# When the weight conversions stand among the attention tiles: a table of 24 steps redrawn

## The chip, the cores and the metric

The kernel runs on one core of one Trainium2 chip. The metric is the device time of one execution in microseconds (us). The core has five engines that run side by side and wait for one another by semaphores: TensorE (PE in the profile; PEld is its weight load), VectorE (DVE), ScalarE (ACT), GpSimd (POOL) and SyncE (SP), which here issues nearly every DMA.

## What is computed

Three layers follow one another, for B = 4 batches of S = 448 tokens with E = 768 channels (12 heads of 64). q, k, v are float32; all weights are float64 in memory.

```python
attn = softmax(causal(q @ k.T / 8)) @ v          # 4 x 12 heads, 448 x 448 scores
x = attn.reshape(B, S, E)
h = relu(x.T @ w_tok1) @ w_tok2                  # token mixing
u = x + h.T
x = u + relu(u @ w_ch1) @ w_ch2                  # channel mixing, 768 -> 1536 -> 768
theta = x @ w_theta                              # third layer
y = w_tok_r @ (x * cos(theta)) + w_tok_i @ (x * sin(theta))
u = x + y
out = u + relu(u @ w_ch)
```

## The kernel before

**Steps.** The attention is cut into 168 steps: 24 pairs of heads (6 to a batch) by 7 tiles of query rows. One pass of the loop over `steps` writes the scores of step n (`scores`, matmuls in L353, and L355 from step 84), the mask and row maximum on DVE (L360), the exponential on ACT (L362), and four steps later (`LAG`) the product with v (`late_step`, L401 or L412). Up to step 55 the probabilities are turned on PE (L369); from step 56 by a DMA transpose from `ph` to `pt` in SP's queue (L385). After every second pair the token mixing runs (L436 to L455).

**Units.** The channel mixing is cut into 96 units of 18 matmuls (L231 to L233): 24 for a batch, of which 0 to 5 and 12 to 17 belong to `w_ch1`, the others to `w_ch2`. Unit 0 starts at step `FIRST_UNIT` = 53; there is a unit about every 2.5 steps up to step 88 and then one about every 1.45 steps, so that unit 23 is due at step 102. A unit's weights are a tile of 384 KB in HBM (`wd`, w_c in the profile), loaded by `load_unit` (L226) up to three units ahead.

**Conversions.** Those 24 tiles must first be made out of the float64 weights, once, in the order of the first 24 units. This is the list `ROUNDINGS`: pairs (step, n), where n < 0 are the four tiles of the token mixing at steps 3, 4, 8, 9, and n = 0 to 23 are the tiles of the channel mixing. A conversion that stands at step s does this:

- step s: `round_first`: the high words are copied on ACT (L177) and their sign is cut out on POOL (L130, `raw`)
- step s + 1: `round_bits`: two bit operations on DVE (L185, L186), and the squares of the rows on ACT (L124)
- step s + 2: the `fetch` of the conversion three places later in the list (L173, 768 KB, 3 `raw` buffers)
- step s + 3: `round_split`: a power of two from the squares (`power`: two matmuls of one column, two DVE operations of one column, L140 and L127, two small POOL operations), then the high part on POOL (L163, `ws`) and the low part on DVE (L197, `ws`)
- step s + 5: `round_store`: the tile goes to HBM (L569, 384 KB). Only then may `load_unit` fetch it for its unit.

**Order.** The order on each engine is fixed when the program is built: a scheduler goes by the order of the code, by priorities (the attention is placed 500 instructions ahead by `AHEAD`, conversions and units are not) and by its own estimate of times. On the chip each engine then takes its instructions strictly in that order, and SP its DMAs too. Six late conversions for `w_ch` (`convert_late`) and the third layer come after step 94 in the code and are not touched.

Of the kernel before, what the change touches and what calls it, by code (L numbers as in the profile page):

```python
# [35 lines left out]
FIRST_UNIT, DENSE, RATE = 53, 88, (42, 29)  # L36
UNIT_STEPS = [FIRST_UNIT + n * (DENSE - FIRST_UNIT) // 14 if n < 14 else
              DENSE + -(-(n - 14) * RATE[0] // RATE[1]) for n in range(72)]
ROUNDINGS = [(at_step, n - 4) for n, at_step in enumerate((3, 4, 8, 9))] + [(14 + n * 78 // 23, n) for n in range(24)]
ENGINES = {  # L40
    0: dict(qhi="A", qlo="D", khi="A", klo="D", v="D", phi="A", xhi="A", xlo="D", uhi="A", ulo="D"),
}
# [12 lines left out]
def fused(ctx, tc, q, k, v, w_tok1, w_tok2, w_ch1, w_ch2, w_theta, w_tok, w_ch, out):  # L55
# [124 lines left out]
    def round64(f, raw):  # L180


        low, sign = raw[:, :f.shape[-1], 0], raw[:, :f.shape[-1], 1]
        u = f.bitcast(U32)
        nc.vector.scalar_tensor_tensor(out=u, in0=u, scalar=3, in1=sign, op0=ALU.logical_shift_left, op1=ALU.bitwise_or)  # L185
        nc.vector.scalar_tensor_tensor(out=u, in0=low, scalar=29, in1=u, op0=ALU.logical_shift_right, op1=ALU.bitwise_or)  # L186
# [74 lines left out]
    def tok_weights(n):  # L261
        if n < 2:
            cols = slice(n * 512, (n + 1) * 512)
            return w_tok1[:, cols], wt1[:, :, cols]
        return w_tok2[:, (n - 2) * S:(n - 1) * S], wt2[:, n - 2]
# [273 lines left out]
    def fetch(j):  # L539
        if j < len(ROUNDINGS):  # L540
            n = ROUNDINGS[j][1]
            src = tok_weights(n + 4)[0] if n < 0 else jobs[n][0]
            fetched[j] = src, raw_tile()
            fetch64(*fetched[j])
# [6 lines left out]
    def round_bits(j):  # L551
        n, f = ROUNDINGS[j][1], rounding[j]
        round64(f, fetched.pop(j)[1])
        if n < 0:
            split_w(tok_weights(n + 4)[1], rounding.pop(j))
        else:
            rounding[j] = f, row_squares(f)

    def round_split(j):
        n = ROUNDINGS[j][1]  # L560
        if n >= 0:
            f, sq = rounding.pop(j)
            rounding[j] = ws_tile()
            split_scaled("P", rounding[j], f, jobs[n][2], sq)

    def round_store(j):
        n = ROUNDINGS[j][1]
        if n >= 0:
            nc.sync.dma_start(out=jobs[n][1], in_=rounding.pop(j))  # L569
            stored.add(n)  # L570
# [65 lines left out]
    for n, (b, pr, t) in enumerate(steps):  # L636
# [6 lines left out]
        if n == 0:  # L643
            for j in range(BUFS["raw"]):
                fetch(j)
        for j, (at_step, _) in enumerate(ROUNDINGS):
            if at_step == n - ROUND_BITS:
# [350 lines left out]
```

## Time and profile before

| | us |
|---|---|
| median of 3 runs (876.57 to 880.31) | 880.0 |
| the profiled execution | 880.48 |
| its span, first to last instruction | 878.7 |

The profiled execution is 0.48 us over the median of the runs; 1.8 us of it lie around the span. The rows below all come from that one execution. In a row of windows, "busy" is the time in which an engine had an instruction running, in us of the window, with the number of instructions behind it; PEclk is the granted clock of TensorE as a share of full speed (1.00 is 2.4 GHz, a half is 1.2 GHz); DMA share is the mean busy share of the 16 DMA engines.

### The profile page before, as it was taken

The numbers are of one execution on the slowest core, as the hardware profiler recorded it, in microseconds if no ns is written. First come the engines' busy times: TensorE is split into PE (matmuls) and PEld (weight loads), VectorE is DVE, ScalarE is ACT, GpSimd is POOL, SyncE is SP. The second block draws the span as 40 slices with busy tenths as digits, with TensorE's granted clock in tenths as the row PEclk, the third lists the DMA queues.
The fourth block names the chain that finished last, engine by engine and source line by source line (L and its number), as shares of the span: only waits on it lengthen the run. The fifth ranks groups of instructions, "written<-read, shape, count | busy, mean of one in ns | idle before, by whom it ended". The sixth has DMA issues, their size and how long they took to land.

```text
span 878.7 us, 16252 instructions
## 1 busy us (share of the span) xinstructions
PE 844.2 (96%) x5603; PEld 532.3 (61%) x5603; DVE 611.8 (70%) x1438; ACT 540.1 (61%) x1271; POOL 255.3 (29%) x445
## 2 busy tenths in 40 slices
PE   7999988998989999999999999999999999999997
PEld 6888865566547566665656555555545555555554
DVE  6788797989997666767785358669737448567441
ACT  6797786676856665567755266547636448456441
POOL 4466564447561201222312035341101001101000
PEclk9999999999999999999999999999999999999999
DMA  7856869899699996765574888612612132131011
GB/s 223 259 194 204 265 164 301 232 337 260 160 323 301 287 212 168 199 174 124 160 210 101 251 278 282 219 36 70 198 39 88 48 100 80 56 117 58 19 50 74
DMA packets 122563, 152.01 MB, mean 173 GB/s; under 512 B 78384, under 2 KB 89584, under 8 KB 122480
## 3 DMA queue, kind: packets, MB, share of 16 engines
q1 hardware_dynamic: 121936, 149.95, 58.8%
q0 software_dynamic: 384, 0.79, 0.4%
q8 instruction: 44, 0.72, 0.4%
q14 instruction: 39, 0.32, 0.1%
q10 hardware_dynamic: 160, 0.23, 0.1%
HBM read 110.56 MB, written 22.81 MB: 152 GB/s over the span
## 4 chain that ended last, share of the span: by engine, by line
PE 70%; DMA 12%; DVE 6%; ACT 5%; issue 3%; POOL 2%; SPq 1%; DVEq 0%; ACTq 0%; POOLq 0%
PE ps_mm L231 16%; PE ps_mm L232 16%; PE ps_mm L233 16%; DMA pt<-ph 8%; PE ps_sc L353 4%; PE ps_sc L231 3%; PE ps_sc L232 3%; PE ps_sc L233 3%; DMA ws<-w_c 2%; PE ps_pv L401 2%; ACT junk L124 2%; PE ps_pv L412 2%; DVE ph L382 1%; PE ps_mm L785 1%; PE ps_mm L369 1%
## 5 line engine op out<-in xcount | busy, mean ns | idle before, releaser
L231 PE MATMUL ps_mm<-h,ws 128*128 128x448 f16 x432 | 153.2, 356 | 3.3 <-POOL h L163 1.7
L232 PE MATMUL ps_mm<-h,ws 128*128 128x448 f16 x432 | 153.3, 356 | 1.1 <-DVE g L127 1.0
L233 PE MATMUL ps_mm<-h,ws 128*128 128x448 f16 x432 | 152.8, 355 | 0.0
L233 PEld LDWEIGHTS <-ws 128*128 128x128 f16 x720 | 70.6, 98 | 66.7 <-issue 6.7
L231 PEld LDWEIGHTS <-ws 128*128 128x128 f16 x720 | 70.7, 98 | 65.4 <-issue 3.8
L232 PEld LDWEIGHTS <-ws 128*128 128x128 f16 x720 | 70.7, 98 | 61.9 <-issue 5.4
L362 ACT ACTIVATE sb<-sb,mx 128x320 f32<-128x320 f32 (+3 forms) x168 | 89.3, 533 | 28.0 <-DVE mx L360 27.3
L232 PE MATMUL ps_mm<-ut,ws 128*128 128x448 f16 x288 | 101.5, 353 | 2.4 <-DVE ut L197 2.4
L231 PE MATMUL ps_mm<-ut,ws 128*128 128x448 f16 x288 | 101.2, 353 | 1.5 <-DMA rawt<-x2d 1.3
L233 PE MATMUL ps_mm<-ut,ws 128*128 128x448 f16 x288 | 101.6, 353 | 0.0
L382 DVE SCALAR_TENSOR_TENSOR ph<-sb,ph 128x64 f16<-128x64 f32 (+3 forms) x208 | 64.5, 353 | 32.1 <-ACT ph L160 31.7
L360 DVE CUSTOM_DVE_ANT_0 sb<-ps_sc,mask 128x320 f32<-128x320 f32 (+3 forms) x168 | 74.5, 454 | 14.8 <-PE ps_mm L369 11.4
L160 ACT ACTIVATE ph<-sb 128x192 f16<-128x192 f32 (+3 forms) x112 | 48.4, 442 | 56.3 <-DMA pt<-ph 55.8
L124 ACT ACTIVATE junk<-acc 128x448 bf16<-128x448 f32 x72 | 41.1, 571 | 65.5 <-DVE acc L890 42.7
L353 PE MATMUL ps_sc<-k_pad,q_raw 128*128 128x192 f32 (+3 forms) x168 | 58.8, 451 | 6.0 <-DMA k_pad<-in_k_dram 4.6
L765 POOL TENSOR_SCALAR tmp<-tmp 128x384 f32<-128x384 f32 x28 | 15.5, 555 | 147.4 <-ACT tmp L764 144.3
L163 POOL TENSOR_SCALAR h<-t 128x448 f16<-128x448 f32 x48 | 33.4, 697 | 79.4 <-ACT t L485 78.8
L487 DVE TENSOR_TENSOR h<-t,h 128x448 f16<-128x448 f32 x48 | 32.1, 672 | 23.8 <-POOL h L163 23.7
L231 PE MATMUL ps_sc<-th,ut 128*128 128x384 f16 x144 | 46.9, 326 | 0.0
L233 PE MATMUL ps_sc<-th,ut 128*128 128x384 f16 x144 | 46.8, 326 | 0.0
L232 PE MATMUL ps_sc<-th,ut 128*128 128x384 f16 x144 | 46.6, 326 | 0.0
L130 POOL TENSOR_SCALAR raw<-raw 128x768 f32<-128x768 f32 (+2 forms) x34 | 34.2, 1006 | 40.1 <-ACT wf L177 36.1
(215 smaller groups left out, 2093.8 us busy)
## 6 DMA issues: line engine op xcount, KB each, us to landing
ws<-w_c SPq DMA_DIRECT2D x120, 384.0 KB, 4.5
raw<-in_w_ch_dram SPq DMA_DIRECT2D x30, 768.0 KB, 6.0
w_c<-ws SPq DMA_DIRECT2D x30, 384.0 KB, 3.9
v_raw<-in_v_dram SPq DMA_DIRECT2D x24, 288.0 KB, 3.8
q_raw<-in_q_dram SPq DMA_DIRECT2D x12, 448.0 KB, 4.4
k_raw<-in_k_dram SPq DMA_DIRECT2D x12, 448.0 KB, 5.0
x2d<-acc SPq DMA_DIRECT2D x24, 224.0 KB, 3.6
acc<-x2d SPq DMA_DIRECT2D x24, 224.0 KB, 2.8
```

The source lines that it names most:

```text
L124: nc.scalar.activation(j[:, 0:src.shape[-1]], src, AF.Square, accum_out=dst)
L130: nc.gpsimd.tensor_scalar(out=dst, in0=a, scalar1=b, scalar2=c, op0=ALU.mult, op1=ALU.mult)
L160: nc.scalar.activation(dst, src, AF.Copy, scale=scale)
L163: e.tensor_scalar(out=dst, in0=src, scalar1=scale, scalar2=0.0, op0=ALU.mult, op1=ALU.add)
L231: nc.tensor.matmul(ps, lhsT=ka(a[:, 0]), rhs=kb(b[:, 0]), start=first, stop=False)
L232: nc.tensor.matmul(ps, lhsT=ka(a[:, 0]), rhs=kb(b[:, 1]), start=False, stop=False)
L233: return nc.tensor.matmul(ps, lhsT=ka(a[:, 1]), rhs=kb(b[:, 0]), start=False, stop=last)
L353: nc.tensor.matmul(ps[:, 0:n], lhsT=lhs, rhs=cut(pp.kh), start=True, stop=pp.kl is None)
L360: pp.first = nc.vector.tensor_tensor_reduce(out=dst, in0=src, in1=msk, op0=ALU.add, op1=ALU.min, scale=-0.125, scalar=3.0e38, accum_out=pp ...
L362: pp.last = nc.scalar.activation(sb[:, 0:kk], sb[:, 0:kk], AF.Exp, bias=pp.mx[:, j:j + 1], scale=-1.0, accum_out=pp.sm[:, 2 + j:3 + j])
L382: nc.vector.scalar_tensor_tensor(out=dst, in0=sb[:, c0:c1], scalar=PSC, in1=hi[:, c0:c1], op0=ALU.mult, op1=ALU.subtract)
L487: gates[0] = nc.vector.tensor_tensor(out=t[:, 1], in0=f, in1=t[:, 0], op=ALU.subtract)
```

## The change

The list of steps for n = 0 to 23 is another one; nothing else is touched. Before, the 24 conversions stand at 14, 17, 20, 24, 27, 30, 34, 37, 41, 44, 47, 51, 54, 58, 61, 64, 68, 71, 75, 78, 81, 85, 88, 92. Now they stand at 12, 14, 17, 19, 22, 24, 27, 29, 32, 34, 37, 39, 42 and then at 44, 49, 54, 59, 64, 69, 74, 79, 84, 89, 94.

```diff
-ROUNDINGS = [(at_step, n - 4) for n, at_step in enumerate((3, 4, 8, 9))] + [(14 + n * 78 // 23, n) for n in range(24)]
+ROUNDINGS = [(at_step, n - 4) for n, at_step in enumerate((3, 4, 8, 9))] + [(12 + n * 5 // 2 if n < 13 else 44 + (n - 13) * 5, n) for n in range(24)]
```

The first place is DVE around step 35, from the end of one pair of heads (L418) to the score tile of step 36 (L360, 128x192). Names: `wf` is the tile under conversion, `ws` its finished form, `h` belongs to the token mixing. Before:

```order
L418 RECIPROCAL sm<-sm 128x7
L185 SCALAR_TENSOR_TENSOR wf<-wf,raw 128x768
L440 SCALAR_TENSOR_TENSOR h_913<-ps_mm,h_913 128x256
L186 SCALAR_TENSOR_TENSOR wf<-raw,wf 128x768
L197 SCALAR_TENSOR_TENSOR ws<-wf,s,ws 128x768
L440 SCALAR_TENSOR_TENSOR h_913<-ps_mm,h_913 128x256
L360 ISA sb_186,mx<-ps_sc,mask 128x192
```

Now, from after the same reciprocal on:

```order
L197 SCALAR_TENSOR_TENSOR ws<-wf,s,ws 128x768
L440 SCALAR_TENSOR_TENSOR h_962<-ps_mm,h_962 128x256
L197 SCALAR_TENSOR_TENSOR ws<-wf,s,ws 128x768
L440 SCALAR_TENSOR_TENSOR h_962<-ps_mm,h_962 128x256
L185 SCALAR_TENSOR_TENSOR wf<-wf,raw 128x768
L186 SCALAR_TENSOR_TENSOR wf<-raw,wf 128x768
L185 SCALAR_TENSOR_TENSOR wf<-wf,raw 128x768
L455 TENSOR_TENSOR acc<-ps_mm,acc 128x448 x2
L140 TENSOR_SCALAR g<-ps_mm 128x1
L186 SCALAR_TENSOR_TENSOR wf<-raw,wf 128x768
L360 ISA sb_186,mx<-ps_sc,mask 128x192
```

Three operations of a conversion stood ahead of that score tile; now there are six, and the two additions of the token mixing (L455) stand ahead of it as well.

The second place is SP's queue at the last conversion, n = 23, whose tile is `w_c2_1_5`. Before, the transposes are those of steps 101 to 104:

```order
L385 DMA_TRANSPOSE pt_3699<-ph_3695 128x5x128
L508 DMA x2d0_1_70<-acc_596 128x448
L569 DMA w_c2_1_5_116<-ws_3457 128x1536
L508 DMA x2d0_2_71<-acc_949 128x448
L508 DMA x2d0_3_72<-acc_966 128x448
L173 DMA raw_6615<-in_w_ch_dram 128x1536
L385 DMA_TRANSPOSE pt_3724<-ph_3720 128x5x128
L385 DMA_TRANSPOSE pt_3843<-ph_3839 128x7x128
L385 DMA_TRANSPOSE pt_3887<-ph_3883 128x7x128
L226 DMA ws_3554<-w_c2_1_5_116 128x1536
```

Now, they are those of steps 104 to 107:

```order
L385 DMA_TRANSPOSE pt_3887<-ph_3883 128x7x128
L508 DMA x2d0_2_71<-acc_998 128x448
L508 DMA x2d0_3_72<-acc_1015 128x448
L385 DMA_TRANSPOSE pt_3943<-ph_3940 128x2x128
L385 DMA_TRANSPOSE pt_3975<-ph_3971 128x3x128
L569 DMA w_c2_1_5_116<-ws_3516 128x1536
L385 DMA_TRANSPOSE pt_4020<-ph_4016 128x3x128
L226 DMA ws_3631<-w_c2_1_5_116 128x1536
```

The store of the last tile stood ahead of step 102's transpose and its load behind step 104's; now the store stands behind step 106's and the load behind step 107's. On PE unit 23 itself stands behind the scores of step 111 before and behind those of step 112 now. Between the scores of step 107 and unit 23, PE has 10 matmuls of unit 22 before, and 40 of units 20 to 22 now. From step 140 on the order on PE is the same in both.

## Rows read from the trace of the kernel before

**Rows 1.** Busy time of each engine by stage (the windows view).

```profile
core 0: us, PE busy (x) PEld busy (x) DVE busy (x) ACT busy (x) POOL busy (x), PEclk, DMA share, GB/s
25.00:82.00 57.00, 56.21 (x408) 49.53 (x407) 45.31 (x118) 47.20 (x132) 32.29 (x47) 1.00 0.69 215
82.00:105.00 23.00, 21.87 (x158) 18.65 (x158) 17.96 (x44) 17.47 (x50) 13.54 (x18) 1.00 0.74 247
105.00:134.00 29.00, 24.41 (x182) 18.40 (x181) 27.05 (x70) 24.14 (x63) 20.08 (x33) 1.00 0.72 181
134.00:160.00 26.00, 23.66 (x159) 14.67 (x158) 20.11 (x64) 17.84 (x50) 11.31 (x19) 0.93 0.98 280
160.00:188.00 28.00, 26.21 (x211) 18.31 (x210) 27.86 (x70) 20.04 (x47) 12.10 (x18) 1.00 1.02 301
188.00:228.00 40.00, 36.27 (x277) 23.21 (x277) 35.99 (x86) 25.09 (x64) 21.10 (x33) 0.91 0.91 245
228.00:264.00 36.00, 32.14 (x213) 17.58 (x212) 34.65 (x79) 25.49 (x60) 24.88 (x33) 0.95 0.91 267
```

**Rows 2.** Windows view of line L362 alone, two ACT records to a step.

```profile
0.00:25.00 25.00, 9.77 (x28) 1.00 0.77 239
25.00:82.00 57.00, 17.25 (x58) 1.00 0.69 215
82.00:105.00 23.00, 6.08 (x21) 1.00 0.74 247
105.00:228.00 123.00, 25.80 (x86) 0.96 0.90 250
```

**Rows 3.** Tile wf, 25 to 82 us: count, duration in ns min/median/max.

```profile
L177 ACT ACTIVATE wf<-raw x9: 898/917/958, 25.5 to 81.0; 128x768 f32<-128x768 f32 x9
L185 DVE SCALAR_TENSOR_TENSOR wf<-wf,raw x8: 952/958/984, 28.0 to 76.7; 128x768 uint32<-128x768 uint32 x8
L186 DVE SCALAR_TENSOR_TENSOR wf<-raw,wf x8: 947/957/1534, 29.0 to 77.6; 128x768 uint32<-128x768 uint32 x8
L124 ACT ACTIVATE junk<-wf x8: 836/844/893, 30.7 to 79.5; 128x768 bf16<-128x768 f32 x8
L163 POOL TENSOR_SCALAR ws<-wf,s x7: 902/907/1645, 38.2 to 79.0; 128x768 f16<-128x768 f32 x7
L197 DVE SCALAR_TENSOR_TENSOR ws<-wf,s,ws x7: 1007/1016/1043, 39.9 to 80.9; 128x768 f16<-128x768 f32 x7
```

**Rows 4.** Groups by line and shape, 25 to 228 us: count, busy us, mean ns.

```profile
L140 DVE TENSOR_SCALAR g<-ps_mm 128x1 uint32<-128x1 uint32 x28 | 4.0, 147 | 1.1 <-PE ps_mm L138 1.1
```

**Rows 5.** DMA issues of the page: count, KB each, us to landing.

```profile
raw<-in_w_ch_dram SPq DMA_DIRECT2D x30, 768.0 KB, 6.0
w_c<-ws SPq DMA_DIRECT2D x30, 384.0 KB, 3.9
```

**Rows 6.** Timeline of DVE around step 35: start, us, instruction, idle before and its releaser.

```profile
65.66 0.96 DVE L185 SCALAR_TENSOR_TENSOR wf<-wf,raw 128x768 uint32<-128x768 uint32 x1 [0.73 <-POOL raw L130]
...
70.94 0.36 DVE L360 CUSTOM_DVE_ANT_0 sb<-ps_sc,mask 128x192 f32<-128x192 f32 x1 [1.23 <-PE ps_mm L369]
```

**Rows 7.** PE's waits, 105 to 228 us: us in total, times, longest.

```profile
PE ps_pv L412 <- DMA pt<-ph: 3.9, 4, 2.0
PE ps_sc L353 <- DVE mx L360: 3.3, 4, 1.9
PE ps_mm L232 <- DVE ut L197: 2.4, 2, 1.2
PE ps_mm L437 <- DVE xg L167: 0.7, 1, 0.7
```

**Rows 8.** Timeline of SP at the last conversion's store and load.

```profile
267.12 0.41 SPq L569 DMA_DIRECT2D w_c<-ws  x1
...
276.11 1.00 SPq L226 DMA_DIRECT2D ws<-w_c  x2
...
283.97 1.18 SPq L385 DMA_TRANSPOSE pt<-ph  x1
```

**Rows 9.** Timeline of PE at the start of unit 23 and three matmuls later.

```profile
280.14 0.36 PE L231 MATMUL ps_mm<-h,ws 128*128 128x448 f16 x1 [0.96 <-DMA ws<-w_c]
...
280.72 0.35 PE L231 MATMUL ps_mm<-h,ws 128*128 128x448 f16 x1
```

## Prediction

> **What bounds the kernel now.** I read the windows view first, cut where the steps of the change lie, then the same view for line L362 alone, which dates the steps, and last the waits of PE. By the count of exponentials [rows 2] 14 steps have begun at 25 us, 43 at 82 us, about 54 at 105 us and about 97 at 228 us. So the 13 dense conversions of the new list (steps 12 to 42) fall into 25 to 82 us, and the stretch that is thinned (steps 53 to 94) is 105 to 228 us.
>
> The two stretches have different limits [rows 1]. From 25 to 82 us PE is busy 56.21 of 57 us at full clock: it sets the pace. DVE has 45.31 of 57, ACT 47.20, the DMA engines 0.69; all have some room, none much. From 105 to 228 us PE is busy 24.41 + 23.66 + 26.21 + 36.27 = 110.6 of 123 us, so it idles 12.4 us, and the clock is 0.93 in 26 us and 0.91 in 40 us, which is worth 1.8 + 3.6 = 5.4 us more. DVE there has 27.05 + 20.11 + 27.86 + 35.99 = 111.0 of 123, and between 160 and 188 us it has no gap at all; the DMA share is 0.98 and 1.02 in 134 to 188 us. What PE waits for there [rows 7] is DVE (row maximum 3.3, `ut` 2.4, `xg` 0.7, in all 6.4 us) and the transposes (3.9 us). So the change takes work from a stretch where DVE and the DMA hold PE up, and puts it where PE holds the others up, as long as they have room.
>
> **What one conversion costs.** On DVE 0.957 + 0.957 (L185, L186) and 1.016 (L197) [rows 3], and two operations of one column at 0.147 [rows 4]: 1.91 us at step s + 1 and 1.31 us at step s + 3. On ACT 0.917 + 0.844. By DMA 768 KB in and 384 KB out [rows 5].
>
> **The dense stretch, 25 to 82 us.** Counted by their own steps, nine pairs of bit operations fall into steps 13 to 42 before and twelve now, eight splits before and twelve now. That is 3 x 1.91 + 4 x 1.31 = 11.0 us more on DVE, which then has 56.3 of 57 us: the cover is just gone. ACT goes from 47.20 to 52.5 with three more pairs of its own. The first place of the change shows how it will bind. Between the reciprocal and the score tile of step 36 DVE idled 0.73 + 1.23 us before [rows 6]; now it has three more operations of conversions (1.016 + 0.957 + 0.957 = 2.9 us), so about 1 us of them is not covered, before anything is said of the two additions that also moved ahead. What is late next is that score tile's row maximum, then its exponential, and then PE for want of a free score bank. For the size I take the nearest row: between 160 and 188 us DVE works 27.86 of 28 and PE 26.21 of 28, so PE idles 6.4% beside a full DVE. At that share of 57 us PE would idle 3.6 us and not 0.8: **+2.8 us**. Bounds: 0, if DVE fits all of it into its gaps; +11.0, if all of it lies end to end on the path. A gain is excluded here, since nothing is taken away and PE has but 0.8 us to give.
>
> **Steps 43 to 52, 82 to 105 us.** Three pairs of bit operations and three splits before, and the same now: nothing.
>
> **The thinned stretch, 105 to 228 us.** Steps 53 to 94 have twelve pairs of bit operations and twelve splits before and eight of each now, one fewer in each of the four windows: 4 x 3.22 = 12.9 us less on DVE, 98 of 123 us, 80%, about the share that DVE has in the early stretch, where PE hardly waits. The fetches go from ten to six and the stores from twelve to nine, 4 x 768 + 3 x 384 KB = 4.2 MB of the 30.8 that 250 GB/s move in 123 us [rows 2], 14%. I take two thirds of the 6.4 us that PE waits for DVE (-4.3), 14% of the 3.9 us for the transposes (-0.5), and one third of the clock's 5.4 us, since the low clock follows PE's idle stretches and a third of these go (-1.8): **-6.6 us**. Bounds: 0, if the freed room is filled by waits for the transposes, and -17.8, all that PE lacks there.
>
> **The tail of the conversions, 228 us and on.** The last conversion stands two steps later, so one pair of bit operations, 1.9 us, moves in here, where DVE is busy 34.65 of 36 us [rows 1]. And SP's queue brings the last tile later. Before, its store is issued at 267.12 and its load at 276.11, the transpose of step 107 at 283.97 [rows 8], and unit 23 starts at 280.14 after 0.96 us of waiting for exactly this load [rows 9]: there is no slack already. Now the load stands behind step 107's transpose, at 283.97 + 1.18 = 285.2 us if these times held, 9.0 us later. Against this PE has 30 more matmuls to do between the scores of step 107 and unit 23, at (280.72 - 280.14) / 3 = 0.19 us each 5.8 us, so unit 23 would wait about 3.2 us more. It is not sure that the transposes keep their distance to the scores with DVE freer; I take two thirds of this, **+2.1 us**, which leaves the 1.9 us of DVE in it. Bounds: -1.0, if the wait of before goes, and +9.0, if the reordering hides nothing. After step 140 PE's order is the same as before, and nothing further is moved.
>
> **Sum.** +2.8 - 6.6 + 2.1 = -1.7 us on the profiled 880.48, so 878.8; the median of the runs is 0.48 us below the profiled execution: **878.3 us**. Half a per cent, 4.4 us, is about what can be told from no change here, the three runs of before lying 3.7 us apart. The likeliest case is therefore no change that can be told.
>
> **Rivals.** *Faster: the thinned stretch gives most of its waits back.* If PE there waited no more than it does from 25 to 82 us (1.4% of 123 us, 1.7 us), at full clock, the gain would be 16 us; with two thirds of that, 11, and the other two terms at +2.8 and +1, the time is 880 - 7 = 873. It decides once that stretch is 9.3 us shorter. For it: DVE has no gap in 160 to 188 us, and its waits and the transposes come one after the other there. Against it: with fewer conversions the share of the DMA engines falls by a seventh only, and a freed DVE wait can turn into a transpose's.
>
> *Slower: DVE becomes the bound from 25 to 82 us.* Place: the score tiles between two dense conversions. The longest L186 lasts 1.534 us against 0.957, the longest L163 on POOL 1.645 against 0.907 [rows 3]: some of these already meet something that nearly doubles them. If the 3 x 2 + 4 = 10 added operations and as many of those already there lasted 0.58 us longer each, DVE would need 56.3 + 11.6 = 68 us in a stretch of 57. Then the stretch is 11 us longer, and with -6.6 and +2.1 the time is 880 + 6.5 = 886. It decides once the stretch has grown by 9 us, which some 17 such meetings make. Against it: the medians of all these rows are the short times.
> The Trainium skill has a rule for this (SBUF — State Buffer, "Who interferes with whom"): a DVE instruction with two SBUF inputs and a GpSimd instruction that reads SBUF contend for one shared pair of ports, and the second to issue is blocked until the first has ended. By that rule two conversions that overlap, as they will at every second or third step, block one another more often, and this rival's 886 would be the forecast; the trace so far agrees in the maxima alone.
>
> *Slower: unit 23 waits out the whole 9.0 us.* With +2.8 and -4 in the thinned stretch that is 880 + 7.8 = 888; it decides once unit 23 waits 5.6 us more than before. For it speaks that the load was late already; against it, the 5.8 us of other matmuls.
>
> **Chances.** No change 0.44 (875.6 to 884.4), faster 0.33, slower 0.23 (DVE in the dense stretch 0.13, unit 23 0.10). The range 868 to 888 takes in two thirds of the thinned stretch's bound with nothing lost elsewhere at its lower end (880 - 12), and the two slower rivals at its upper; the likeliest case alone has 875 to 884.
>
> **What would show it.** In the windows of the changed kernel: DVE at or over 54 of 57 us while the first 43 steps run, and step 43 begun 2 to 4 us later; DVE near 80% and fewer stretches of low clock while steps 53 to 94 run; SP's load of the last tile right ahead of unit 23, and PE's wait for it. Wrong would be the forecast if PE stays at 98% in the dense stretch with DVE full, if the thinned stretch stays as long with its waits going to the transposes, or if unit 23 waits over 5 us.

## The result and the profile after

The changed kernel takes 887.8 us in the median of six runs (886.86 to 889.47), the kernel before 880.2 beside it: a ratio of 1.0098, with an interval of 1.0075 to 1.0120. It is slower, by more than the half per cent that can be told. The profiled execution took 889.47 us, its span is 887.7, so 9.0 us more than the span before; it was the longest of the six, and the medians are 7.6 us apart.

The first view is that of the windows, cut at the same times as [rows 1].

```profile
core 0: us, PE busy (x) PEld busy (x) DVE busy (x) ACT busy (x) POOL busy (x), PEclk, DMA share, GB/s
25.00:82.00 57.00, 50.92 (x361) 44.72 (x360) 46.86 (x115) 45.14 (x121) 31.91 (x49) 0.98 0.80 241
82.00:105.00 23.00, 21.23 (x148) 18.16 (x149) 19.19 (x49) 19.91 (x53) 16.91 (x24) 0.98 0.74 240
105.00:134.00 29.00, 27.67 (x186) 21.26 (x186) 25.83 (x66) 24.64 (x65) 19.54 (x31) 1.00 0.82 272
134.00:160.00 26.00, 24.13 (x203) 17.27 (x202) 21.29 (x66) 19.45 (x55) 13.65 (x20) 1.00 0.97 233
160.00:188.00 28.00, 24.78 (x199) 15.96 (x198) 25.17 (x69) 17.35 (x45) 13.37 (x21) 1.00 0.92 242
188.00:228.00 40.00, 34.78 (x267) 24.42 (x265) 33.38 (x88) 26.24 (x67) 15.02 (x27) 0.96 0.97 240
228.00:264.00 36.00, 33.57 (x257) 20.57 (x255) 33.51 (x78) 24.79 (x57) 15.13 (x24) 1.00 0.96 259
264.00:310.00 46.00, 40.63 (x311) 26.39 (x312) 31.91 (x90) 30.04 (x80) 11.26 (x22) 1.00 0.96 275
```

What PE loses in a window is its idle time and the share of the clock that is not granted. From 25 to 82 us that was 0.8 us before [rows 1]; now it is 6.1 + 0.02 x 57 = 7.2, so 6.4 more, although DVE is busy only 46.86 of 57 us. From 105 to 228 us it was 12.4 + 5.4 = 17.8; now it is 11.6 idle and 0.04 x 40 = 1.6 of clock, 13.2, so 4.6 less. From 228 to 264 us it falls from 5.7 to 2.4. From 264 to 310 us it rises from 1.0 (PE busy 45.04 of 46 before) to 5.4. Equal times are not equal steps, though: at 105 us 50 steps have begun and not 53 as before, at 228 us 95 in both.

The second view is the same, cut at the first exponential (L362) of steps 14, 28, 36 and 43, so that the same steps stand in each row: 30, 17 and 15 records of that line in both kernels. First the kernel before, then the changed one.

```profile
25.10:53.30 28.20, 27.88 (x203) 24.68 (x202) 20.18 (x54) 22.92 (x65) 14.31 (x21) 1.00 0.67 203
53.30:71.70 18.40, 17.93 (x132) 15.83 (x130) 15.36 (x37) 13.88 (x39) 11.51 (x16) 1.00 0.75 243
71.70:82.70 11.00, 11.00 (x80) 9.41 (x80) 10.09 (x31) 11.00 (x34) 6.86 (x13) 1.00 0.70 209
```

```profile
27.10:57.60 30.50, 27.98 (x206) 24.62 (x205) 24.32 (x64) 25.44 (x70) 15.63 (x27) 1.00 0.79 228
57.60:81.30 23.70, 20.14 (x138) 17.53 (x139) 20.95 (x49) 16.90 (x46) 15.33 (x22) 0.96 0.77 254
81.30:92.70 11.40, 10.57 (x71) 9.09 (x70) 8.30 (x22) 9.88 (x29) 7.99 (x12) 0.93 0.64 185
```

Steps 14 to 42 take 57.6 us before and 65.6 now, 8.0 more; 5.3 of these fall into steps 28 to 35, around one run of the token mixing. PE itself loses 4.0 us more in them (3.6 idle and 0.9 by the clock now, 0.5 idle before); the rest is work of its own that stands there now. DVE has 20.95 us to do in them, 5.6 more than before. (In steps 14 to 27, 2.3 us longer, PE's waits are for ScalarE, 1.6 us in all, and for a fill by GpSimd, 0.8. The 2.0 us by which step 14 begins later are mostly not the change's: in e9, e11 and e12 below, with the same list up to step 84, it begins at 25.1 to 26.7 us, and at 25.1 before.) What waits in these 23.7 us the view of the waits shows (the engine and tile that waited, for whom, total us, times, longest).

```profile
POOL raw L130 <- ACT wf L177: 3.6, 2, 1.8
ACT wf L177 <- DVE ws L197: 3.5, 3, 1.6
POOL p_w L130 <- DVE g L140: 3.2, 2, 2.9
DVE ws L197 <- POOL ws L163: 2.4, 3, 1.3
PEld ps_mm L369 <- DVE acc L455: 2.4, 1, 2.4
PE ps_mm L369 <- DVE acc L455: 2.1, 1, 2.1
```

And DVE's own timeline before the score tile of step 36, the first place of the change:

```profile
70.74 1.02 DVE L197 SCALAR_TENSOR_TENSOR ws<-wf,s,ws 128x768 f16<-128x768 f32 x1 [0.62 <-POOL ws L163]
...
73.36 1.61 DVE L197 SCALAR_TENSOR_TENSOR ws<-wf,s,ws 128x768 f16<-128x768 f32 x1 [1.27 <-POOL ws L163]
...
76.20 1.52 DVE L186 SCALAR_TENSOR_TENSOR wf<-raw,wf 128x768 uint32<-128x768 uint32 x1
77.64 0.95 DVE L185 SCALAR_TENSOR_TENSOR wf<-wf,raw 128x768 uint32<-128x768 uint32 x1
78.51 1.14 DVE L455 TENSOR_TENSOR acc<-ps_mm,acc 128x448 f32<-128x448 f32 x2
...
80.51 0.34 DVE L360 CUSTOM_DVE_ANT_0 sb<-ps_sc,mask 128x192 f32<-128x192 f32 x1
```

The score tile that began at 70.94 us [rows 6] begins at 80.51. With its 2.4 us of waits for GpSimd's high parts DVE has 23.35 of the 23.7 us taken: it has no time left there, while over the whole dense stretch it seems to have a fifth. Its 5.6 us more are, nearly all, one pair of bit operations and one split more that fall into these steps by the new list (3.2), the two additions, of which only 0.3 us stood ahead of this cut before (1.14 - 0.3), and long operations: the 1.61 and 1.52 us in the rows above and an L197 of 1.65 at 61.62 us, where before there was one of 1.53 (some 1.2 net). PE meets this at the two additions L455, for which its next transposes wait:

```profile
79.18 1.06 PE L369 MATMUL ps_mm<-ident,sb 128*128 128x128 f32 x5 [2.13 <-DVE acc L455]
```

Right behind this wait, at 79.5 us, the granted clock falls to a half for 3.4 us (hence 0.96 and 0.93 in the rows above, where it was 1.00 before).

In the tail, SP brings the last tile as the prediction said, the load behind the store and step 107's transpose:

```profile
277.22 0.32 SPq L569 DMA_DIRECT2D w_c<-ws  x1
277.65 1.20 SPq L385 DMA_TRANSPOSE pt<-ph  x1
279.67 3.30 SPq L226 DMA_DIRECT2D ws<-w_c  x7
```

But PE doesn't wait for it. These are all its waits from 260 to 388 us:

```profile
PE ps_pv L412 <- DMA pt<-ph: 5.4, 5, 2.4
PE ps_sc L353 <- DVE mx L360: 3.0, 3, 1.1
PE ps_mm L231 <- DVE h L440: 1.7, 1, 1.7
PE ps_pv L412 <- DVE v_raw L321: 0.5, 1, 0.5
```

Step 104 to the first exponential of step 130 takes 263.8 to 344.8, 81.0 us, before, and 260.6 to 353.7, 93.1 us, now. The windows of line L231 say where the work went; with L232 and L233 it holds the matmuls of all the units, and a few of the token mixing. From step 112 to 130, before and now:

```profile
290.30:344.80 54.50, 24.05 (x68) 7.10 (x69) 1.00 0.87 215
```

```profile
287.10:353.70 66.60, 28.32 (x80) 8.15 (x79) 0.97 0.73 202
```

Twelve more, and eleven more in L232 and in L233, so about two units' worth came later than before against the scores; seven of the twelve stood in steps 104 to 111 before (29 there, 22 now). With the same cuts, what PE loses between steps 104 and 130, all engines counted, first before, then now:

```profile
263.80:290.30 26.50, 25.54 (x203) 18.19 (x202) 17.94 (x51) 17.50 (x51) 4.08 (x8) 1.00 1.11 312
290.30:344.80 54.50, 53.64 (x410) 34.26 (x410) 35.97 (x106) 30.40 (x81) 8.46 (x18) 1.00 0.87 215
```

```profile
260.60:287.10 26.50, 21.67 (x168) 15.02 (x167) 19.80 (x53) 16.95 (x47) 5.02 (x10) 1.00 0.93 222
287.10:353.70 66.60, 62.59 (x474) 39.67 (x473) 41.38 (x113) 34.30 (x92) 13.16 (x23) 0.97 0.73 202
```

Now that is 4.8 + 4.0 idle and 2.0 of clock, 10.8 us; before it was 26.5 - 25.54 and 54.5 - 53.64, 1.8 us. So of the 12.1 us more 9.0 are lost, and 3.1 are work that stood ahead of step 104 before. From there to the end of the attention (120.5 us before, 121.6 now) and in the third layer nothing of size is added: step 167 begins 10.0 us later, the end comes 9.0 us later. In sum, steps 14 to 42 lose some 8 us, the thinned stretch up to 264 us gives some 8 back, and 9 are lost behind it.

### The profile page after: what moved, and what is told of

The parts are those of the page before. It is cut to its first block, busy times and chain, and to the rows that moved or that the text cites. A ratio compares the mean times of both kernels' runs of the same rounds, so it can differ in the third digit from the quotient of the medians.

```text
span 887.7 us, 16258 instructions
## 1 busy us (share of the span) xinstructions
PE 840.3 (95%) x5603; PEld 533.1 (60%) x5603; DVE 610.5 (69%) x1438; ACT 541.6 (61%) x1271; POOL 247.6 (28%) x445
## 4 chain that ended last, share of the span: by engine, by line
PE 65%; DMA 13%; DVE 9%; ACT 5%; issue 3%; POOL 3%; SPq 1%; ACTq 0%; DVEq 0%; POOLq 0%
PE ps_mm L231 15%; PE ps_mm L232 15%; PE ps_mm L233 15%; DMA pt<-ph 6%; PE ps_sc L353 3%; PE ps_sc L231 3%; PE ps_sc L233 3%; PE ps_sc L232 3%; DMA q_raw<-in_q_dram 2%; PE ps_pv L401 2%; ACT junk L124 2%; PE ps_pv L412 1%; DVE ph L382 1%; DVE wf L185 1%; DVE sb L360 1%
## 5 line engine op out<-in xcount | busy, mean ns | idle before, releaser
L232 PE MATMUL ps_mm<-h,ws 128*128 128x448 f16 x432 | 151.9, 352 | 1.2 <-DVE h L487 1.2
L231 PE MATMUL ps_mm<-h,ws 128*128 128x448 f16 x432 | 151.8, 353 | 1.1 <-DVE acc L455 0.9
L233 PE MATMUL ps_mm<-h,ws 128*128 128x448 f16 x432 | 151.8, 353 | 0.0
L231 PEld LDWEIGHTS <-ws 128*128 128x128 f16 x720 | 70.4, 98 | 63.9 <-issue 3.1
L233 PEld LDWEIGHTS <-ws 128*128 128x128 f16 x720 | 70.4, 98 | 63.8 <-issue 3.4
L232 PEld LDWEIGHTS <-ws 128*128 128x128 f16 x720 | 70.4, 98 | 61.4 <-issue 4.1
L362 ACT ACTIVATE sb<-sb,mx 128x320 f32<-128x320 f32 (+3 forms) x168 | 89.2, 533 | 24.0 <-DVE mx L360 21.8
L231 PE MATMUL ps_mm<-ut,ws 128*128 128x448 f16 x288 | 101.2, 353 | 2.0 <-DMA rawt<-x2d 1.4
L232 PE MATMUL ps_mm<-ut,ws 128*128 128x448 f16 x288 | 101.8, 353 | 0.1
L233 PE MATMUL ps_mm<-ut,ws 128*128 128x448 f16 x288 | 101.8, 353 | 0.0
L382 DVE SCALAR_TENSOR_TENSOR ph<-sb,ph 128x64 f16<-128x64 f32 (+3 forms) x208 | 63.4, 348 | 34.8 <-ACT ph L160 34.4
L360 DVE CUSTOM_DVE_ANT_0 sb<-ps_sc,mask 128x320 f32<-128x320 f32 (+3 forms) x168 | 74.0, 454 | 11.2 <-PE ps_mm L369 3.8
L124 ACT ACTIVATE junk<-acc 128x448 bf16<-128x448 f32 x72 | 41.2, 573 | 65.6 <-DVE acc L890 40.8
L163 POOL TENSOR_SCALAR h<-t 128x448 f16<-128x448 f32 x48 | 31.8, 663 | 100.8 <-ACT t L485 100.4
L487 DVE TENSOR_TENSOR h<-t,h 128x448 f16<-128x448 f32 x48 | 32.5, 680 | 25.1 <-POOL h L163 24.7
L130 POOL TENSOR_SCALAR raw<-raw 128x768 f32<-128x768 f32 (+2 forms) x34 | 32.7, 962 | 56.7 <-ACT wf L177 44.7
L231 PE MATMUL ps_sc<-th,ut 128*128 128x384 f16 x144 | 46.9, 326 | 0.0
L233 PE MATMUL ps_sc<-th,ut 128*128 128x384 f16 x144 | 46.8, 326 | 0.0
L232 PE MATMUL ps_sc<-th,ut 128*128 128x384 f16 x144 | 46.6, 326 | 0.0
```

Of the source, the lines that this page charges most:

```text
L124: nc.scalar.activation(j[:, 0:src.shape[-1]], src, AF.Square, accum_out=dst)
L130: nc.gpsimd.tensor_scalar(out=dst, in0=a, scalar1=b, scalar2=c, op0=ALU.mult, op1=ALU.mult)
L163: e.tensor_scalar(out=dst, in0=src, scalar1=scale, scalar2=0.0, op0=ALU.mult, op1=ALU.add)
L231: nc.tensor.matmul(ps, lhsT=ka(a[:, 0]), rhs=kb(b[:, 0]), start=first, stop=False)
L232: nc.tensor.matmul(ps, lhsT=ka(a[:, 0]), rhs=kb(b[:, 1]), start=False, stop=False)
L233: return nc.tensor.matmul(ps, lhsT=ka(a[:, 1]), rhs=kb(b[:, 0]), start=False, stop=last)
```

## The experiments

Each expectation is the text on record. Its theories are these. **A**: the dense stretch costs its microseconds by its density, through the engines that take their work in order; its variants name the link (A1 the three `wf` buffers, A2 two conversions that meet in one step, A3 GpSimd, A4 ScalarE, A5 the very steps on which it falls). **B**: the last conversions, two steps later, cost what is lost behind 264 us (B1 the last, B2 the one before it). **C**: any redrawing of the list moves the time either way, by the order that comes out of it. **D**: the cost goes by how far the units fall behind the score steps in PE's order.

The kernel before had medians of 877.9 to 880.4 us beside them, so small differences are to be read from the ratios. A stage's time comes from one execution, and holds work that another list has moved into it as well as what is lost.

This table has all of them (us; the median, its ratio to the kernel before in the same batch with the interval, and from the profiled execution the time from the first exponential of step 14 to that of 43, of 43 to 104, and of 104 to 130).

| | median | ratio | 14-43 | 43-104 | 104-130 |
|---|---|---|---|---|---|
| before | 880.2 | | 57.6 | 181.1 | 81.0 |
| changed | 887.8 | 1.0098 (1.0075-1.0120) | 65.6 | 167.9 | 93.1 |
| e1 | 893.8 | 1.0144 (1.0114-1.0173) | 67.2 | 184.5 | 81.2 |
| e2 | 888.5 | 1.0099 (1.0074-1.0123) | 61.5 | 179.9 | 84.8 |
| e3 | 898.1 | 1.0203 (1.0174-1.0231) | 66.8 | 182.2 | 86.5 |
| e4 | 891.0 | 1.0131 (1.0103-1.0158) | 60.1 | 171.9 | 93.5 |
| e5 | 889.0 | 1.0106 (1.0083-1.0130) | 57.6 | 187.3 | 84.9 |
| e6 | 881.2 | 1.0018 (1.0003-1.0033) | 60.6 | 182.7 | 79.1 |
| e7 | 887.7 | 1.0102 (1.0076-1.0127) | 64.9 | 172.3 | 84.7 |
| e9 | 881.0 | 1.0012 (0.9987-1.0037) | 65.1 | 172.2 | 78.2 |
| e10 | 882.3 | 1.0048 (1.0028-1.0067) | 57.6 | 180.4 | 84.4 |
| e11 | 885.9 | 1.0076 (1.0050-1.0103) | 64.5 | 170.6 | 87.8 |
| e12 | 886.6 | 1.0092 (1.0071-1.0113) | 65.8 | 168.7 | 89.6 |
| e13 | 893.7 | 1.0168 (1.0142-1.0194) | 62.2 | 181.3 | 87.8 |
| e14 | 881.0 | 1.0030 (1.0014-1.0046) | 59.9 | 175.2 | 83.0 |
| e15 | 892.4 | 1.0165 (1.0133-1.0196) | 60.4 | 178.4 | 91.6 |
| e16 | 887.9 | 1.0116 (1.0085-1.0147) | 64.6 | 169.2 | 88.8 |
| e17 | 885.7 | 1.0074 (1.0045-1.0102) | 63.4 | 170.1 | 90.3 |
| e18 | 888.6 | 1.0139 (1.0074-1.0203) | 62.0 | 175.8 | 89.2 |
| e19 | 885.1 | 1.0080 (1.0056-1.0105) | 65.2 | 175.3 | 80.0 |

**e1: the dense part alone**, the later eleven as before.

```diff
-[(12 + n * 5 // 2 if n < 13 else 44 + (n - 13) * 5, n) for n in range(24)]
+[(12 + n * 5 // 2 if n < 13 else 14 + n * 78 // 23, n) for n in range(24)]
```

> The first thirteen conversions stand as in the changed kernel (12 to 42), the last eleven as in the kernel before (58 to 92). Theory A (the dense stretch itself costs: conversions that stand ahead of score tiles on DVE and ACT make PE wait): step 44 begins some 10 us later than before, as in the changed kernel, and since steps 58 to 92 are as full as before, only the gap at 43 to 57 gives back; 886 to 892 us. Theory B (the loss of the changed kernel is made after step 100, by the two steps that the last conversions stand later): the tail stands as before, so 878 to 882 us. Theory C (any redrawing of the order costs or gains some us by chance): anything from 874 to 890 with no tie to the dense stretch.

893.8 us is a little over A's 886 to 892, and B alone (878 to 882) is out. Steps 14 to 43 lose 9.6 us. The dense part costs that by itself, and without the thinning nothing comes back. Steps 43 to 104 take 184.5 us, 16.6 more than in the changed kernel, which in its turn has put off units and takes 11.9 more behind step 104 (93.1 against 81.2). The difference, 4.7 us, is the thinning's worth seen from the other side.

**e2: every third step, then every fourth.**

```diff
+[(12 + n * 3 if n < 13 else 52 + (n - 13) * 4, n) for n in range(24)]
```

> A mild form: every third step from 12 to 48, then every fourth from 52 to 92. Theory A: eleven conversions in steps 12 to 42 and not nine or thirteen, so step 44 begins 3 to 6 us later than before, and of that most comes back behind step 52; 878 to 883 us. Theory B: 878 to 882. Theory C: anything from 874 to 890.

888.5 us misses A (878 to 883) and B (878 to 882) by over 5 us. The dense loss is 3.9 us and the gain behind it 1.2. Half the density costs half as much, but gives nearly nothing back.

**e3: the changed list, its last eleven drawn together to end at 92** (44, 48, 53, 58, 63, 68, 72, 77, 82, 87, 92).

```diff
+[(12 + n * 5 // 2 if n < 13 else 44 + (n - 13) * 48 // 10, n) for n in range(24)]
```

> The changed kernel with its last eleven conversions at 44, 48, 53, 58, 63, 68, 72, 77, 82, 87, 92 and not 44 to 94: the last stands where it stood before. Theory A: the dense stretch is unchanged, 886 to 890 us. Theory B: 879 to 883 us, with no waits of PE after step 104 that the kernel before has not. Theory C: anything from 874 to 890.

It was meant to take the lateness out, and is the slowest of all: steps 43 to 104 take 182.2 us where the changed kernel takes 167.9, with the same number of conversions on steps a place or two apart. It misses A (886 to 890) and B (879 to 883) and falls to C, which names no cause.

**e4: the changed list, its first fourteen a step later** (13, 15, 18, ... 43, 45, then 49, 54, ... 94 as in the changed kernel; the expectation counts more of them as moved).

```diff
+[(13 + n * 5 // 2 if n < 13 else 45 + (n - 13) * 49 // 10, n) for n in range(24)]
```

> The changed list with all but the last five conversions one step later (13 to 43, then 45 to 94). Nothing is denser or thinner than in the changed kernel, so theories A and B both say 886 to 890 us. Theory C: a shift by one step redraws the order as much as any other edit, and the time lies anywhere from 876 to 892; a time under 883 speaks for it.

The dense stretch costs 2.5 us instead of 8, with the same thirteen conversions; the end, at 94 again, costs as much as in the changed kernel (93.5 us), and steps 43 to 104 give 4.0 us less back. So the 891.0 us, near the 886 to 890 of A and B, are made of other parts than theirs.

**e5 and e6: the even list a step earlier, and a step later.**

```diff
-[(14 + n * 78 // 23, n) for n in range(24)]
+[(13 + n * 78 // 23, n) for n in range(24)]
```

> The even list of the kernel before, every conversion one step earlier (13 to 91): as dense as before everywhere. Theory A (density in steps 12 to 42 costs, lateness at the end costs) says 878 to 882 us, as before. Theory C (the order of before is a lucky one, and any redrawing loses it, whatever its density) says 886 to 894, since four redrawn lists so far lay at 888 to 898.

> The even list, every conversion one step later (15 to 93). Theory A: early stretch as before; the last conversion one step later than before costs 1 to 4 us after 264 us, so 880 to 885. Theory C: 886 to 894.

Neither changes a density. One costs 1.1%, as C says, the other 0.2%, as A says. So an order can be a per cent worse for no reason that a count of the work shows, and the kernel before is a good draw.

**e7: four `wf` buffers** in the changed kernel (`t` goes to 2 to make room).

```diff
-BUFS = dict(ut=12, h2=8, acc=12, ws=8, wf=3, raw=3, sb=3, ph=3, pt=5, t=3, junk=1)
+BUFS = dict(ut=12, h2=8, acc=12, ws=8, wf=4, raw=3, sb=3, ph=3, pt=5, t=2, junk=1)
```

> The changed kernel with four buffers for the tile under conversion (wf) and not three, paid for with two buffers for t and not three (t is used by the units, from step 53 on alone). Theory A1 (in the dense stretch ACT waits for a free wf buffer, which DVE's split frees, which waits for POOL): ACT's wait for L197 is gone and the lag at step 42 shrinks from 10 us to 3 to 6. Theory A2 (it is the time on DVE itself that makes score tiles late): the lag stays at 9 to 11 us. The total says less, since t costs units something; 880 to 892 us.

ScalarE's wait for L197 is gone from the list of waits, the loss in the dense stretch is not: 64.9 us. A1 is wrong. With the same late end, steps 104 to 130 take 84.7 us here and not 93.1, and the whole takes as long, so the late end has no fixed price at that place.

**e9: the changed list with its last two conversions at 88 and 92**, where the kernel before has them.

```diff
+[(12 + n * 5 // 2 if n < 13 else (44 + (n - 13) * 5 if n < 22 else 88 + (n - 22) * 4), n) for n in range(24)]
```

> The changed kernel with its last two conversions at 88 and 92, as before, and not at 89 and 94. Theory A with lateness: the dense stretch costs its 10 us up to step 42 as in the changed kernel, the stretch behind 264 us no longer costs 9 us but 0 to 3, so 879 to 884 us. If the loss behind 264 us does not come of the two late steps, 886 to 890. Theory C: anything from 876 to 898.

881.0 us: 6.8 us come back, nearly all that was lost. (The two profiled executions lie 10.6 us apart, so their stages show more than the medians.) The dense stretch is as slow as ever (65.1 us), steps 43 to 104 give 8.9 us back, and steps 104 to 130 take 78.2 us instead of 93.1. PE's waits there, to be held against those of the changed kernel above:

```profile
PE ps_pv L412 <- DMA pt<-ph: 3.8, 4, 1.3
PE ps_sc L353 <- DVE mx L360: 0.5, 1, 0.5
```

and its windows from step 104 to 112 and to 130:

```profile
262.90:281.10 18.20, 16.89 (x133) 12.32 (x132) 15.07 (x45) 13.01 (x38) 0.90 (x3) 1.00 1.08 344
281.10:341.10 60.00, 57.53 (x440) 36.58 (x439) 38.99 (x109) 33.45 (x90) 12.58 (x23) 1.00 0.80 213
```

PE loses 1.3 + 2.5 = 3.8 us there, the changed kernel 10.8.

**e10, e11, e12: the tail by halves.** The kernel before with its last two at 89 and 94; the changed one with 89 and 92, and with 88 and 94.

```diff
+[((89, 94)[n - 22] if n > 21 else 14 + n * 78 // 23, n) for n in range(24)]
+[(12 + n * 5 // 2 if n < 13 else (44 + (n - 13) * 5 if n < 23 else 92), n) for n in range(24)]
+[(12 + n * 5 // 2 if n < 13 else (44 + (n - 13) * 5 if n != 22 else 88), n) for n in range(24)]
```

> The even list of before, with its last two conversions at 89 and 94 where they stood at 88 and 92: the tail of the change alone. Theory B (the late end of the list costs what is lost behind 264 us): 880 + 7, the difference of the changed kernel and of the one with 88 and 92 (887.8 - 881.0), so 886 to 889. Theory D (what costs is how far the units fall behind the score steps; on PE unit 30 stands behind step 125 here, behind 119 before, 127 in the changed kernel): some 6/8 of that, 885. Theory C (any redrawing moves the time either way by chance): anything between 878 and 890, with the loss not behind 264 us.

> The changed list with its last conversion alone back at 92 (89, 92). If the loss behind 264 us hangs on the last conversion (theory B1): 881, like the kernel with 88 and 92. If it hangs on the one before it, n = 22 (theory B2): 888. Theory D: unit 30 stands behind step 125 on PE (124 with 88 and 92, 127 in the changed kernel), so near 883.

> The changed list with n = 22 alone back at 88 (88, 94). Theory B1: 888, as the last conversion still stands at 94. Theory B2: 881. Theory D: unit 30 stands behind step 127 and unit 23 behind 114, so 888 or more.

On the even list the late end costs 3.4 us. In the profiled execution, its longest with 885.0 us, steps 104 to 130 take 3.4 us more, the place that B names, and those from there to step 167 take 3.6 more, which nobody had forecast. B's 886 to 889 is missed: from this side it is half as large as from the other. In the changed list either late conversion alone costs most of the loss against e9 (e11 4.9 us, e12 5.6, both 6.8): neither B1 nor B2. e11's profiled execution took 880.83 us, its shortest, so its row in the table is on the short side. D gave 885, 883 and 888 for the three, within 3 us each time, but e10 and e11 the wrong way round.

**e13: the split two steps after the conversion's place** for the first 13, so that it never shares a step with the bit operations of the next.

```diff
-if at_step == n - ROUND_SPLIT:
+if at_step == n - (2 if 4 <= j < 17 else ROUND_SPLIT):
```

> The changed list with the split of the first 13 conversions two steps after their place and not three, so that the splits (14, 16, 19, 21, ...) never share a step with the bit operations of the next ones (13, 15, 18, 20, ...), which in the changed kernel they do at every fifth step. If the loss of 8 to 11 us before 82 us comes from two conversions meeting in one step (theory A2): at most 4 us are lost by step 43, and the time is near 882 if the tail stays as it is. If it comes from the number of conversions alone (theory A): 8 to 11 us are lost by then, and the time is 886 to 890. Against A2 stands that the power of two is then wanted two steps after the squares' words, so waits for ACT may come in their place.

The dense stretch costs 4.6 us and not 8, near the bound set for A2. The time is worse all the same, since the steps from 43 to 104 give nothing back (181.3). A2 is not settled by it.

**e14: e4 with the last two at 88 and 92.**

```diff
+[(13 + n * 5 // 2 if n < 13 else (45 + (n - 13) * 49 // 10 if n < 22 else 88 + (n - 22) * 4), n) for n in range(24)]
```

> The dense stretch one step later (13 to 43), with the last two conversions at 88 and 92. If the parts add up (theories A and B): the dense stretch loses 4 us as it did with 89 and 94 (891.0), the tail 5 to 7 us less than there, so 884 to 886; with the changed list's gain in the thinned stretch on top, 880. Theory D: unit 30 stands behind step 125, so 883 to 886. Theory C: no sum holds, anything between 878 and 892.

The profiled execution loses 2.3 us in the dense stretch, gets 5.9 back in the thinned one and loses 2.0 in the tail, 1.6 us less in all than before. The median, 881.0 us, is still 0.3% over the kernel before beside it, and the best of the dense lists with e9. It is near the 880 at the end of the expectation, but the tail takes 10.5 us less than in e4, not 5 to 7. In steps 28 to 35 DVE is as full as in the changed kernel, but has 2.0 us less to do:

```profile
54.90:75.70 20.80, 19.08 (x136) 16.54 (x136) 18.91 (x46) 17.80 (x47) 15.15 (x21) 1.00 0.83 283
```

18.91 us, and 1.5 of waits for GpSimd's high parts, fill 20.4 of 20.8 us. Less work by 2.0 and less waiting by 0.9 are the whole 2.9 us by which these steps are shorter than in the changed kernel.

**e15, e16, e17: one engine's share of a dense conversion left out**, in the changed kernel.

```diff
-        round64(f, fetched.pop(j)[1])
+        raw = fetched.pop(j)[1]
+        if not 0 <= n < 13:
+            round64(f, raw)
...
-            rounding[j] = f, row_squares(f)
+            rounding[j] = f, ones[:, 0:1] if n < 13 else row_squares(f)
...
-        product(high, high, 0.0, 1.0)
+        if not bare:
+            product(high, high, 0.0, 1.0)
```

> The changed kernel without the two bit operations on DVE (L185, L186) in the first 13 conversions, so their sign and their last three bits are left out; 1.9 us less of DVE for each. If DVE's time and place in its order make the loss before 82 us (theory A): the loss at 82 us falls from 7 to 10 us to 0 to 3, and the time to 879 to 882. If it is the chain through ScalarE and GpSimd (theories A3, A4): the loss stays at 5 or more, 885 to 888.

> The changed kernel without the squares on ScalarE (L124, 0.84 us each) in the first 13 conversions; their power of two is that of a column of ones. If ScalarE's time makes the loss before 82 us (theory A4): the loss at 82 us falls to 0 to 3 us, 879 to 882. Theory A and A3: it stays at 7 to 10 us, 886 to 889.

> The changed kernel without the sign's cut on GpSimd (L130) in the first 13 conversions, so that their weights have other high bits. If GpSimd's link between ScalarE's copy and DVE's bit operations makes the loss before 82 us (theory A3: raw waits for the copy and DVE for raw): the loss at 82 us falls to 0 to 3 us, 879 to 882. Theory A: DVE has as much to do as before, the loss stays at 5 to 10 us, 885 to 889.

Without DVE's bit operations the dense stretch loses 2.8 us, without the squares 7.0, without the sign's cut 5.8. The changed kernel and e9, e11 and e12, whose lists are the same up to step 84, lose 8.0, 7.5, 6.9 and 8.2, which is how far one execution tells. So it is DVE's part that holds the others up; neither A3 nor A4 makes the loss, though the cut, 1.1 us under the lowest of the four, may have a small share. With the bit operations gone DVE has room in steps 28 to 35:

```profile
53.10:75.00 21.90, 19.97 (x139) 16.75 (x138) 12.84 (x40) 16.94 (x48) 12.22 (x21) 1.00 0.82 292
```

PE loses 1.9 us in them, where the changed kernel lost 4.5. They still take 3.5 us more than before, since PE has 2.0 us more of its own work there. The forecast of the time was wrong, though: 892.4 us with less to do. Steps 104 to 130 take 10.6 us more than before, with 3.0 us in one wait of PE for a unit's weights. Less work, in another order, took longer: C again.

**e18 and e19: the dense stretch from 14, and from 11**, with the end at 88 and 92.

```diff
+[(14 + n * 5 // 2 if n < 13 else (46 + (n - 13) * 19 // 4 if n < 22 else 88 + (n - 22) * 4), n) for n in range(24)]
+[(11 + n * 5 // 2 if n < 13 else (44 + (n - 13) * 5 if n < 22 else 88 + (n - 22) * 4), n) for n in range(24)]
```

> The dense stretch from step 14 to 44, the last two conversions at 88 and 92. Steps 14 to 43 took 57.6 us before, 65.6 in the changed kernel and 60.1 with the dense stretch at 13 to 43. If its density costs the 8 us (theory A): 64 to 66 us again, and 883 to 886. If it is the steps on which it falls, and the density alone is worth about the forecast 2.8 us (theory A5): 59 to 62 us, and 878 to 882.

> The dense stretch from step 11 to 41, the last two conversions at 88 and 92. Theory A: steps 14 to 43 take 64 to 66 us, and the time is 883 to 886. Theory A5: 59 to 62 us, and 878 to 882.

From 11 the stretch takes 65.2 us and the time is 885.1, as A says. From 14 it takes 62.0, the upper end of A5, and the time misses both by a loss in steps 104 to 130 (89.2 us) that e9, with the same end, does not have. Steps 28 to 35 are where it is lost again, as these two rows show:

```profile
53.40:76.20 22.80, 18.84 (x133) 15.96 (x133) 19.81 (x43) 16.60 (x44) 13.90 (x20) 1.00 0.72 228
```

```profile
55.10:81.50 26.40, 20.98 (x149) 17.92 (x148) 23.50 (x52) 18.34 (x49) 16.28 (x24) 1.00 0.62 219
```

The four starts 11, 12, 13 and 14 cost 7.6, 8.0, 2.3 to 2.5, and 4.4 us. DVE's work in steps 28 to 35 orders what these steps take: 18.91, 19.81, 20.95 and 23.50 us of it go with 20.8, 22.8, 23.7 and 26.4 us, 1.9 to 3.0 us above it each time, as before (15.36 and 18.4). In the other runs the steps last 0.8 to 4.4 us longer than DVE's work in them. Only e15 is outside this (12.84 and 21.9 us): with so little for DVE to do, PE's own 19.97 us set the time. So, where DVE has its conversions, the steps last as long as its work and some 3 us more, and A and A5 are both half right: the density brings the work, and the steps on which it falls say how much of it meets the token mixing.

## Why the prediction was wrong

**The dense stretch: the step that failed first.** The prediction put DVE's work on a stretch of 57 us, found 56.3, and read PE's loss, +2.8 us, from another stretch in which DVE was as full. It measured 8.0. DVE did become the bound, but not over the stretch that the sum was made on. The larger part of the loss stands at one place, steps 28 to 35, where the token mixing's own work on DVE meets the conversions; there DVE was busy or waiting for GpSimd for 23.35 of 23.7 us, while over the whole stretch it had a fifth free. The prediction had this place before its eyes, six operations ahead of a score tile where three had stood and the two additions with them, and gave it "about 1 us". The place alone came to 5.3 us. The path was another one, too: the prediction had PE wait for a score bank behind a late row maximum, but for row maxima it waited 0.6 us in steps 14 to 42, and its longest wait, 2.1 us, was that of the transposes for the two additions, which the sum left out. e15 supports that it is DVE's work: without the bit operations 2.8 us are lost and not 8.0, and in steps 28 to 35 PE loses 1.9 us and not 4.5. That +2.8 us was within the spread of starts (2.3 to 8.0 us) is no merit of the argument: with the even list one step later these steps take 3.0 us more with nothing denser, of which PE idles 0.6.

**Steps 43 to 52: nothing.** Right: PE lost 1.1 us in these steps before and 1.2 now. They take 3.2 us longer (22.8 and 26.0), with more of PE's own work in them (159 and 181 matmuls).

**The thinned stretch: right.** -6.6 was forecast; from 105 to 228 us PE lost 4.6 us less, and up to 264 us another 3.3. (Steps 53 to 94 took 13.5 us less, 110.7 and not 124.2, but some 9 of these are work of PE that stands in the steps on either side now.) The split of the term was off. The idle time fell from 12.4 to 11.6 us only, and the clock gave 3.8 us, twice the term for it. PE's waits for the transposes went from 3.9 [rows 7] to 4.9 us:

```profile
PE ps_pv L412 <- DMA pt<-ph: 4.9, 3, 3.1
PE ps_mm L445 <- ACT t L485: 2.4, 1, 2.4
PE ps_sc L353 <- DVE mx L360: 2.1, 2, 1.9
```

(the first three rows of PE's waits from 115 to 228 us, nearly the same steps). So the freed DVE time did go partly into transposes, as was said against the faster rival, and into a wait for ScalarE that was not there before.

**The tail: wrong by its mechanism and its size.** Unit 23 did not wait for its weights; PE waited 1.0 us for them before and not at all now. Of the two slower rivals of the forecast, the one on unit 23 gave 888, the measured time, by a wait that is not there, which is luck. What is late is the order: with the last two conversions one and two steps later, PE's fixed order has unit 23 and those behind it later against the scores (unit 30 stands behind the scores of step 127 now, of 119 before), the scores run ahead, and the units that are left over meet the transposes and the row maxima of steps 112 to 130. The late end costs 3.4 us on the even list (e10) and 6.8 on the changed one (e9), against +2.1. That the shift of the units is the cause of the loss, and not only goes with it, is argued and not shown: e18 has the end at 88 and 92, and its steps 104 to 130 took 8.2 us more too, of which PE lost 4.9. Over all the traces, unit 30 stands behind step 119 to 124 in four kernels, which take 78.2 to 84.8 us for steps 104 to 130, behind 125 in nine (80.0 to 91.6) and behind 126 or 127 in seven (86.5 to 93.5). Its place goes with the time and does not settle it. The sentence that PE's order is the same from step 140 on was wrong as well; it differs to step 156. It did no harm, as step 130 to 167 took 1.1 us more.

**The slower rival on DVE's long operations.** It had the bound and the place right, and the price from the wrong cause. Over steps 14 to 42 of the changed kernel the times of the conversion's operations are

```profile
L185 DVE SCALAR_TENSOR_TENSOR wf<-wf,raw x11: 935/946/960, 27.7 to 88.3; 128x768 uint32<-128x768 uint32 x11
L186 DVE SCALAR_TENSOR_TENSOR wf<-raw,wf x11: 943/958/1573, 29.8 to 89.7; 128x768 uint32<-128x768 uint32 x11
L163 POOL TENSOR_SCALAR ws<-wf,s x10: 903/908/1607, 39.5 to 90.5; 128x768 f16<-128x768 f32 x10
L197 DVE SCALAR_TENSOR_TENSOR ws<-wf,s,ws x10: 1003/1017/1743, 41.2 to 92.8; 128x768 f16<-128x768 f32 x10
```

The medians are those of [rows 3]; only a few near double, and in steps 28 to 35 these made some 1.2 of the 5.6 us. In e14, which lost 2.3 us, L163 has a median of 1.199 and a longest of 2.382 us. The long ones are no measure of the loss. They do begin inside an operation of GpSimd: the L197 at 73.36 us began 0.07 us after GpSimd's L130 (73.29 to 74.17) and ended 0.80 us behind its end. The rule of the Trainium skill that stood beside this rival (SBUF — State Buffer, "Who interferes with whom") agrees with the single long ones and did not decide here.

**What stays open.** A list drawn another way moved the time by about 1% against what its counts say, to the slow side in e3, e5, e15 and e18. A shift of the even list by one step (e5) so costs more than the two late conversions do (e9 against the changed kernel), and part of what e9 gives back may be of this kind. The loss then stands mostly between steps 43 and 104 or between 104 and 130. Which feature of an order makes it was not found; D came within 3 us in e10 to e12, and misses e3 (unit 30 behind step 127 as in the changed kernel, 898.1 us) and e18. Why PE waits for ScalarE and GpSimd in steps 14 to 27 was not traced further. No list tried beats the kernel before.

## What to carry to other kernels

Where engines take their work in a fixed order, a share of busy time over a long stretch says nothing about the place where a rare, heavy job meets the moved work: cut the windows at that job's own steps, and count what stands in the queue ahead of the instruction that PE waits for. Price a change of order first by its neighbours: the same list shifted by one step cost from 0.2% to 1.1% here, so that a gain worked out as a fifth of a per cent could not be promised. And when an early job is made early to free a later stretch, look at what its last one does: two late conversions of 24 went with a loss of 6.8 us, most of what the thinning had given.

## What the hardware showed that was not expected

GpSimd's L163 lasted up to 2.382 us in e14, against 0.901 at its shortest, where [rows 3] had 1.645 as the longest. And leaving out 26 DVE operations of 0.95 us made the kernel slower than leaving them in, 892.4 us against 887.8 in the medians (1.0165 and 1.0098 of the kernel before beside them).
